# Spectral and attention layers in turn: table load, key maximum and value evictions rearranged at the end of the projections, and constant matmuls added there and in attention's first six steps

## The chip, the cores and the metric

The kernel runs on one core of a Trainium2 chip. The metric is the device time in microseconds (us) of one launch, from the first instruction to the last with what lies around it. Five engines work beside each other, each through its own instruction queue in order: TensorE (PE) multiplies matrices into PSUM, VectorE (DVE) and ScalarE (ACT) do elementwise work and carry PSUM into SBUF, GpSimd (POOL) does elementwise work in SBUF, and SyncE (SP) issues DMAs. They wait for each other by semaphores.

## The reference

The input `x` has 2048 rows of 512. Four layers follow each other, A, B, A, B, each added to `x` after a layer norm. A is a spectral filter, B an attention of 32 query heads with one shared key head and value head of 16 columns:

```python
def _A_ref(x, w_r, w_i):
    X = rfft2(x.astype(float32)) * (w_r + 1j * w_i)
    return irfft2(X, s=(S, D)).astype(bfloat16)

def _B_ref(x, wq, wk, wv, wo):
    q = (x @ wq).reshape(B, S, H, Dh).transpose(0, 2, 1, 3)
    k, v = x @ wk, x @ wv
    p = softmax(einsum("bhqd,bkd->bhqk", q, k) * Dh ** -0.5)
    o = einsum("bhqk,bkd->bhqd", p, v)
    return o.transpose(0, 2, 1, 3).reshape(B, S, H * Dh) @ wo

x = x + _A_ref(_layernorm(x), A_w_r, A_w_i)
x = x + _B_ref(_layernorm(x), B_wq, B_wk, B_wv, B_wo)
x = x + _A_ref(_layernorm(x), A_w_r, A_w_i)
x = x + _B_ref(_layernorm(x), B_wq, B_wk, B_wv, B_wo)
```

## The kernel before

The launch runs `spectral_layer` and `attention_layer` twice. `x` stays in SBUF as 16 tiles of 128 x 512, indexed (r, t).

**End of the spectral layer.** `back_s(t)` (L375) writes the four tiles of row block t: 16 matmuls of 128 x 512, an add to `x`, and a layer norm of two tiles at a time (L119), whose normalised tiles `xn_sb` come from ACT or POOL. The row blocks t = 0 to 3 are followed, one behind, by `block(t)` (L450), which makes the attention's inputs from row block t: 16 transposes in two halves into PSUM (L455), copied to `xT` by ACT (first half, L458) and DVE (second half, L460); four matmuls for the keys (L464), evicted to `KT` by ACT (L465); the largest absolute key per row, `kmax`, by DVE from `KT` (L466); 16 small matmuls for the values (L471), evicted four times, scaled, by ACT (L476) and DVE (L478) in turn. `block(0)` also makes the first two query groups. All its PSUM tiles come from one pool of two slots, `psum_b`, used in turn, so a tile waits until the tile two before it has been read. After `block(3)` comes `close` (L485): an exponential on one element (it makes ACT load its exponential table, L487), the maximum over the four `kmax` columns (L488), a scale (L489), and the scaling of all of `KT` in place in two pieces (L491).

**Attention.** The scores are made transposed: 128 keys by 512 queries per tile. A group g is 4 heads of one block of 512 queries; there are 32 groups of 64 score tiles. Each score matmul uses 32 rows of the array, one row strip per head (L569), and each product with the values 32 columns, one column strip per head (L681). Work is written out as 514 steps (L702). In a step, `dve_step` makes one score tile `dv` in PSUM, which DVE turns into integers (`t_new`, L693), and from step 4 on DVE also makes one image `s_new` of four tiles (L699); `act_step` makes three score tiles in one PSUM tile `sc` (two buffers, L663) and ACT takes the exponential of all three (`e`, L669); `pv_step` multiplies what was made two steps earlier with the values. `dv` has one PSUM buffer, so the next `dv` waits for the `t_new` before it. Group 0 takes 18 steps (17 of three tiles and one of one), later groups 16. Two steps after a group's end its sum is evicted by DVE (L584), and queries for the group after next are projected (L441, L446, L447).

**What sets the order.** Ahead of attention a scheduler orders each engine's instructions; within attention `chain` (L509) fixes the order as written. PE takes its instructions in that order, so a matmul that waits holds all behind it.

Of the kernel before, what the change touches and what calls it, by code (L numbers as in the profile page):

```python
# [9 lines left out]
ACT = mybir.ActivationFunctionType  # L10
ALU = mybir.AluOpType
P = 128
BF = mybir.dt.bfloat16
F32 = mybir.dt.float32
I32 = mybir.dt.int32
S, D, H, DH = 2048, 512, 32, 16
NF = D // 2 + 1
NT = 16
NC = 4
R = 4  # L20
T = 4
# [179 lines left out]
def spectral_layer(nc, tc, tabs, shared, lnpool, x_sb, xn_sb, WT, WX, aw, nxt, loads):  # L201
# [5 lines left out]
    with (tc.tile_pool(name="workA", bufs=1) as work,  # L207
# [210 lines left out]
        prep = attention_inputs(nc, tabs, shared, xn_sb, aw)  # L418
        for t in range(T):
            back_s(t)  # L420
            if t > 0:
                prep["block"](t - 1, psum_b)
        prep["block"](T - 1, psum_b)
        prep["close"](xn_sb[:, R - 1, T - 1, 0:1])
    return prep


def attention_inputs(nc, tabs, shared, xn_sb, aw):

    wq_sb, wka, wv_sb, vaug = aw["wq"], aw["wk"], aw["wv"], aw["vaug"]  # L430
    xT = [shared.tile([P, NC, 4, P], BF, tag=f"big{q}", bufs=1, name="xT") for q in range(NQB)]
    KT = shared.tile([P, S], BF, tag="KT", bufs=1)
    kmax = shared.tile([P, NQB], F32, tag="kmax", bufs=1)
    kb = shared.tile([P, 2], F32, tag="kb", bufs=1)
    xTq = [x.rearrange("d c t p -> d c (t p)") for x in xT]
    QT = {}

    def qproj(g, ps):
        qb, hg = divmod(g, HG)
        for c in range(NC):  # L440
            nc.tensor.matmul(ps, lhsT=wq_sb[:, c, hg, :], rhs=xTq[qb][:, c, :],  # L441
                             start=(c == 0), stop=(c == NC - 1))

    def qevict(ps):
        qt = shared.tile([P, 512], BF, tag="QT", bufs=3)
        nc.vector.tensor_copy(out=qt, in_=ps)  # L446
        nc.vector.tensor_tensor(out=qt.bitcast(I16), in0=qt.bitcast(I16), in1=tabs["QAND"], op=ALU.bitwise_and)  # L447
        return qt

    def block(t, psum):  # L450
        for half in range(2):
            ps = psum.tile([P, 2, NC, P], BF, tag="mm")
            for i in range(2):
                for c in range(NC):
                    nc.tensor.transpose(ps[:, i, c, :], xn_sb[:, 2 * half + i, t, c * P:(c + 1) * P], tabs["ident"])  # L455
            dst = xT[t][:, :, 2 * half:2 * half + 2, :].rearrange("d c i p -> d i c p")
            if half == 0:
                nc.scalar.copy(out=dst, in_=ps)  # L458
            else:
                nc.vector.tensor_copy(out=dst, in_=ps)  # L460
        ks = slice(t * 512, (t + 1) * 512)
        ps = psum.tile([P, 512], F32, tag="mm")
        for c in range(NC):
            nc.tensor.matmul(ps, lhsT=wka[:, c, :], rhs=xTq[t][:, c, :], start=(c == 0), stop=(c == NC - 1))  # L464
        nc.scalar.copy(out=KT[:, ks], in_=ps)  # L465
        nc.vector.tensor_reduce(out=kmax[:, t:t + 1], in_=KT[:, ks], axis=mybir.AxisListType.X,  # L466
                                op=ALU.max, apply_absolute_value=True)
        psv = psum.tile([P, 4, DH], F32, tag="mm")
        for i in range(4):
            for c in range(NC):  # L470
                nc.tensor.matmul(psv[:, i, :], lhsT=xT[t][:, c, i, :], rhs=wv_sb[:, c, :],  # L471
                                 start=(c == 0), stop=(c == NC - 1))
        for j in range(4):
            dst = vaug[:, j, 4 * t:4 * t + 4, 0:DH]
            if j % 2 == 0:
                nc.scalar.mul(out=dst, in_=psv, mul=PH_W[j])  # L476
            else:
                nc.vector.tensor_scalar(out=dst, in0=psv, scalar1=PH_W[j], scalar2=None, op0=ALU.mult)  # L478
        if t == 0:
            for g in range(2):  # L480
                ps = psum.tile([P, 512], F32, tag="mm")
                qproj(g, ps)
                QT[g] = qevict(ps)

    def close(xn_last):  # L485
        dmyo = shared.tile([P, 1], F32, tag="dmyo", bufs=1)
        nc.scalar.activation(out=dmyo, in_=xn_last, func=ACT.Exp)  # L487
        nc.vector.tensor_reduce(out=kb[:, 0:1], in_=kmax, axis=mybir.AxisListType.X, op=ALU.max)  # L488
        nc.vector.tensor_scalar(out=kb[:, 1:2], in0=kb[:, 0:1], scalar1=tabs["KAB"][:, 1:2], scalar2=None, op0=ALU.mult)  # L489
        for a, b in ((0, 512), (512, S)):  # L490
            nc.vector.tensor_scalar(out=KT[:, a:b], in0=KT[:, a:b], scalar1=tabs["KAB"][:, 0:1], scalar2=kb[:, 1:2],  # L491
                                    op0=ALU.mult, op1=ALU.add)

    return {"xT": xT, "KT": KT, "QT": QT, "qproj": qproj, "qevict": qevict, "block": block, "close": close}


def attention_layer(nc, tc, tabs, shared, lnpool, x_sb, xn_sb, aw, prep, nxt, store):
    with ExitStack() as ctx:
# [4 lines left out]
        xT, KT, QT = prep["xT"], prep["KT"], prep["QT"]  # L503
        qproj, qevict = prep["qproj"], prep["qevict"]

        mark, last = [None], {}
# [40 lines left out]
        for n0 in range(s0[NG]):  # L547
            lst = []
            if n0 in d_phase:
                g, b, j = d_phase[n0]  # L550
# [3 lines left out]
            n = n0 + LAG  # L554
# [9 lines left out]
        psp = ctx.enter_context(tc.tile_pool(name="psp", bufs=1, space=bass.MemoryType.PSUM))  # L564
        pv, tb, sb, ex, otc = {}, {}, {}, {}, {}

        def score(dst, g, kc, h):
            hs = slice(32 * h, 32 * h + 32)
            nc.tensor.matmul(dst, lhsT=KT[hs, kc * P:(kc + 1) * P], rhs=QT[g][hs, :], start=True, stop=True)  # L569
# [9 lines left out]
        def later(steps, fn):  # L579
            todo.setdefault(now[0] + steps, []).append(fn)  # L580

        def evict(g):
            o = work.tile([P, 512], F32, tag="oraw")
            nc.vector.tensor_copy(out=o, in_=pv.pop(g))  # L584
            d1 = dram.tile([4, 512], F32, tag="d1")
            nc.sync.dma_start(out=d1, in_=o.rearrange("(h r) q -> h r q", r=32)[:, 16, :])
            den = work.tile([P, 16], F32, tag="den")
            nc.sync.dma_start(out=den, in_=d1.rearrange("h (i c) -> (h i) c", c=16))
            return o, den
# [10 lines left out]
        def invert_later(g, o, den):  # L600
            rb = invert(den)
            later(6, lambda: normalise(g, o, rb))
# [57 lines left out]
        def act_step(n):  # L660
            if n >= s0[NG]:
                return
            sc = psc.tile([P, 3, 512], F32, tag="sc")  # L663
            for i, (g, kc, h) in enumerate(act_tiles[n]):
                score(sc[:, i, :], g, kc, h)
            na = len(act_tiles[n])
            e = work.tile([P, 3, 512], BF, tag="e", bufs=7)
            ex[n] = e
            nc.scalar.activation(out=e[:, 0:na, :], in_=sc[:, 0:na, :], func=ACT.Exp, scale=SCALE)  # L669
# [15 lines left out]
        def dve_step(n):  # L685
            if n in d_score:
                g, kc = d_score[n]
                dv = psd.tile([P, 512], F32, tag="dv")
                score(dv, g, kc, kc % 4)
                if kc % 4 == 0:  # L690
                    t_new = work.tile([P, 4, 512], I16, tag="T", bufs=3)
                    tb[(g, kc // 4)] = t_new
                nc.vector.tensor_scalar(out=tb[(g, kc // 4)][:, kc % 4, :], in0=dv, scalar1=T_MUL, scalar2=T_ADD,  # L693
                                        op0=ALU.mult, op1=ALU.add)
            if n in d_phase:
                g, b, j = d_phase[n]
                s_new = work.tile([P, 4, 512], I16, tag="S", bufs=7)
                sb[(g, b, j)] = s_new
                image[0] = nc.vector.tensor_scalar(out=s_new, in0=tb[(g, b)], scalar1=0.5, scalar2=16384.0 + PH_OFF[j],  # L699
                                                   op0=ALU.mult, op1=ALU.add)  # L700

        for n in range(s0[NG]):  # L702
            now[0] = n
            for fn in todo.pop(n, ()):
                fn()
            if n in evict_at:
                o, den = evict(evict_at[n])
                later(4, lambda g=evict_at[n], o=o, den=den: invert_later(g, o, den))
            dve_step(n)
            act_step(n)  # L710
            if n in qproj_at:
                ps = psp.tile([P, 512], F32, tag="pv")
                qproj(qproj_at[n], ps)
                later(1, lambda g=qproj_at[n], ps=ps: QT.__setitem__(g, qevict(ps)))
            else:
                pv_step(n)
            if nxt is not None and n in qproj_at and qproj_at[n] in (11, 15):
                nxt["load"](qproj_at[n] // 4 - 2)
            chain()
# [234 lines left out]
```

## Time and profile before

| | us |
|---|---|
| median of 3 runs (lowest to highest) | 1675.91 (1675.52 to 1676.21) |
| the profiled execution | 1673.17 |
| its span, first to last instruction | 1671.4 |
| PE busy in the span | 1421.6 (85%) |
| DVE busy | 1551.7 (93%) |
| ACT busy | 1505.6 (90%) |
| POOL busy | 158.4 (9%) |
| first score matmul of the first attention | 122.98 |
| first score matmul of the second attention | 947.67 |

All other times in this document that name a moment count from the start of the span. A matmul's shown duration holds its latency; four in a row on PE overlap. An engine's row in the chart of slices is its busy share in tenths, and PEclk is the TensorE clock that was granted, in tenths of full speed.

### The profile page before, as it was taken

The page shows a single profiled execution, that of the slowest core. Times are in us where ns is not written, and L with a number is a line of the kernel's source. Part 1 is how long each engine was busy: PE and PEld are TensorE (multiplying, and loading weights), DVE is VectorE, ACT ScalarE, POOL GpSimd, SP SyncE. Part 2 cuts the span into 40 slices and gives each one's busy share as a digit, 9 for nine tenths or more (in the row PEclk, how much of TensorE's full clock was granted, in tenths as well). Part 3 has the DMA queues.
Part 4 walks back from the last instruction along what each step waited for, and adds up shares of the span by engine and source line. Part 5 has one row for each costly group of instructions (what it writes and reads, how often), then busy time and mean ns, then how long its engine had stood idle before and what let it go on. Part 6 is the DMA issues. An engine that isn't in the chain of part 4 may idle for free.

```text
span 1671.4 us, 32246 instructions
## 1 busy us (share of the span) xinstructions
PE 1421.6 (85%) x12756; PEld 459.7 (28%) x12756; DVE 1551.7 (93%) x2796; ACT 1505.6 (90%) x1250; POOL 158.4 (9%) x264
## 2 busy tenths in 40 slices
PE   7889888888888888888988798888888888888887
PEld 2331222222222222222333322222222222222222
DVE  6877999999999999999878689999999999999994
ACT  4358999999999999999843699999999999999994
POOL 3210000000000000000111100000000000000000
PEclk9896999999999999999999789999999999999999
DMA  7000000000000010000020000000000000000002
GB/s 276 2 1 4 14 16 17 17 16 17 17 17 16 16 29 16 17 17 28 24 70 1 1 8 17 17 16 17 17 16 16 17 15 15 14 16 17 16 17 65
DMA packets 47880, 40.26 MB, mean 24 GB/s; under 512 B 30832, under 2 KB 36208, under 8 KB 47472
## 3 DMA queue, kind: packets, MB, share of 16 engines
q1 hardware_dynamic: 47728, 38.19, 7.7%
q8 instruction: 100, 1.64, 0.4%
q14 instruction: 52, 0.43, 0.1%
HBM read 33.04 MB, written 3.15 MB: 22 GB/s over the span
## 4 chain that ended last, share of the span: by engine, by line
DVE 39%; ACT 24%; PE 18%; issue 17%; DMA 1%; POOL 1%; SPq 0%; POOLq 0%; DVEq 0%; ACTq 0%
ACT e L669 23%; DVE t_new L693 15%; DVE s_new L699 12%; PE pv_new L681 6%; PE dv L569 3%; PE sc L569 2%; DVE o L584 2%; DVE qt L446 2%; PE fd L275 2%; DVE qt L447 2%; PE ps L192 1%; DVE stats L125 1%; PE ps L367 1%; PE ps L379 1%; DVE den L592 1%
## 5 line engine op out<-in xcount | busy, mean ns | idle before, releaser
L669 ACT ACTIVATE e<-sc 128x1536 bf16<-128x1536 f32 (+1 forms) x1028 | 1386.4, 1526 | 16.0 <-PE sc L569 15.5
L693 DVE TENSOR_SCALAR t_new<-dv 128x512 int16<-128x512 f32 x1016 | 695.0, 684 | 35.8 <-PE sc L569 14.5
L699 DVE TENSOR_SCALAR s_new<-t_new 128x2048 int16<-128x2048 int16 x1016 | 698.3, 688 | 0.0
L569 PE MATMUL dv<-qt,KT 32*128 32x512 bf16 x1016 | 389.2, 383 | 121.8 <-DVE t_new L693 114.0
L569 PE MATMUL sc<-qt,KT 32*128 32x512 bf16 x3080 | 421.6, 389 | 36.5 <-ACT e L669 3.2
L681 PE MATMUL pv_new<-s_new,vaug 128*32 128x512 bf16 x4064 | 412.0, 393 | 27.0 <-DVE qt L446 27.0
L681 PE MATMUL pv_new<-e,vaug 128*32 128x512 bf16 x3080 | 408.7, 385 | 0.4 <-ACT e L669 0.4
L569 PEld LDWEIGHTS <-KT 32*128 32x128 bf16 x4096 | 201.2, 91 | 730.1 <-issue 714.9
L681 PEld LDWEIGHTS <-vaug 128*32 128x32 bf16 x7144 | 135.6, 94 | 276.1 <-issue 262.5
L625 POOL TENSOR_TENSOR ot_new<-o,rb 128x176 bf16<-128x176 f32 (+1 forms) x96 | 55.7, 582 | 706.8 <-DVE s_new L699 649.9
L625 POOL TENSOR_TENSOR od<-o,rb 128x176 bf16<-128x176 f32 (+1 forms) x90 | 49.6, 551 | 597.6 <-DVE s_new L699 597.6
L441 PE MATMUL ps<-xT,wq_sb 128*128 128x512 bf16 x256 | 66.3, 381 | 10.8 <-DVE o L584 10.8
L275 PE MATMUL fd<-X,tab_DT 128*128 128x512 bf16 x256 | 56.1, 379 | 2.8 <-DVE X L242 2.8
L279 ACT CAST xn_sb<-fd 128x512 bf16<-128x512 f32 x32 | 18.8, 586 | 40.7 <-PE fd L275 40.7
L446 DVE CAST qt<-ps 128x512 bf16<-128x512 f32 x64 | 44.2, 691 | 0.8 <-PE ps L441 0.8
L584 DVE COPY o<-pv_new 128x512 f32<-128x512 f32 x64 | 43.8, 684 | 0.1
L367 PE MATMUL ps<-tab_PS,st 128*128 128x512 bf16 x128 | 32.8, 416 | 13.0 <-DVE st L315 12.0
L373 ACT CAST U<-ps 128x512 bf16<-128x512 f32 x24 | 14.1, 587 | 29.8 <-PE ps L367 29.8
L125 DVE BATCH_NORM_STATS2 stats<-x_sb 128x6 f32<-128x512 bf16 x48 | 31.8, 677 | 7.2 <-ACT x_sb L383 3.7
L441 PEld LDWEIGHTS <-wq_sb 128*128 128x128 bf16 x256 | 24.6, 96 | 39.7 <-issue 16.0
L275 PEld LDWEIGHTS <-tab_DT 128*128 128x128 bf16 x256 | 24.8, 98 | 32.8 <-issue 3.6
L379 PE MATMUL ps<-U,IT 128*128 128x512 bf16 x128 | 33.2, 379 | 0.0
(133 smaller groups left out, 567.2 us busy)
## 6 DMA issues: line engine op xcount, KB each, us to landing
rb<-d SPq DMA_DIRECT2D x256, 64.0 KB
FT<-const_FT SPq DMA_DIRECT2D x8, 512.0 KB
IT<-const_IT SPq DMA_DIRECT2D x8, 512.0 KB
x_sb<-in_A_x_dram SPq DMA_DIRECT2D x4, 512.0 KB
out_dram<-x_sb SPq DMA_DIRECT2D x16, 128.0 KB
ot_new<-od SPq DMA_DIRECT2D x120, 16.0 KB
wr_raw<-in_A_w_r_dram SPq DMA_DIRECT2D x1, 1028.0 KB
wi_raw<-in_A_w_i_dram SPq DMA_DIRECT2D x1, 1028.0 KB
```

The source lines that it names most:

```text
L275: nc.tensor.matmul(pss[i], lhsT=DT[:, b, w, 128 * fb:128 * fb + 128], rhs=X[:, b, part, c, :, :].rearrange("p k j -> p (k j)"), start=(b = ...
L367: nc.tensor.matmul(ps, lhsT=st[c][:, t, vec, q, fb, :], rhs=PS[:, fb, w, :], start=(k == 0), stop=(k == 3))
L379: nc.tensor.matmul(ps, lhsT=IT[:, t, part, c, r * P:(r + 1) * P], rhs=U[:, t, part, c, :], start=(k == 0), stop=(k == 3 and r % 2 == 1))
L441: nc.tensor.matmul(ps, lhsT=wq_sb[:, c, hg, :], rhs=xTq[qb][:, c, :], start=(c == 0), stop=(c == NC - 1))
L446: nc.vector.tensor_copy(out=qt, in_=ps)
L569: nc.tensor.matmul(dst, lhsT=KT[hs, kc * P:(kc + 1) * P], rhs=QT[g][hs, :], start=True, stop=True)
L584: nc.vector.tensor_copy(out=o, in_=pv.pop(g))
L625: pace(nc.gpsimd.tensor_tensor(out=dst[:, a:b], in0=o[:, a:b], in1=rb[:, a:b], op=ALU.mult))
L669: nc.scalar.activation(out=e[:, 0:na, :], in_=sc[:, 0:na, :], func=ACT.Exp, scale=SCALE)
L681: nc.tensor.matmul(pv[g][32 * h:32 * h + 32, :], lhsT=vaug[:, max(j, 0), kc, :], rhs=rhs, start=(first_pv[(g, h)] == u), stop=(last_pv[(g, ...
L693: nc.vector.tensor_scalar(out=tb[(g, kc // 4)][:, kc % 4, :], in0=dv, scalar1=T_MUL, scalar2=T_ADD, op0=ALU.mult, op1=ALU.add)
L699: image[0] = nc.vector.tensor_scalar(out=s_new, in0=tb[(g, b)], scalar1=0.5, scalar2=16384.0 + PH_OFF[j], op0=ALU.mult, op1=ALU.add)
```

## The change

In `block`, the maximum over the keys reads the PSUM tile, not the SBUF copy. `close` moves into `block(3)`, ahead of the value evictions, and its table-loading exponential reads a piece of `xT` that ACT has copied, in place of the last normalised tile. In `block(3)` a helper `filler` issues matmuls of the identity with data that lies there, into a PSUM tile that nobody reads: 6, 6 and 12. In attention's steps 1 to 5, 4, 3, 3, 2 and 2 such matmuls are written into the `sc` tile just ahead of the three score matmuls that overwrite it, and after step 1 four more into a `pv` tile. The core of the diff:

```diff
         for t in range(T):
             back_s(t)
             if t > 0:
                 prep["block"](t - 1, psum_b)
-        prep["block"](T - 1, psum_b)
-        prep["close"](xn_sb[:, R - 1, T - 1, 0:1])
+        prep["block"](T - 1, psum_b, psum)
...
+    def filler(psum, rhs, n):
+        ps = psum.tile([P, 512], F32, tag="pa", name="idle")
+        for _ in range(n):
+            nc.tensor.matmul(ps, lhsT=tabs["ident"], rhs=rhs, start=True, stop=True)
+
+    def close(last):
+        dmyo = shared.tile([P, 1], F32, tag="dmyo", bufs=1)
+        nc.scalar.activation(out=dmyo, in_=last, func=ACT.Exp)
...
-    def block(t, psum):
+    def block(t, psum, psum_idle=None):
+        if psum_idle is not None:
+            filler(psum_idle, xn_sb[:, 0, t, :], 6)
...
             if half == 0:
                 nc.scalar.copy(out=dst, in_=ps)
+                if psum_idle is not None:
+                    filler(psum_idle, xT[t][:, 0:2, 0:2, :], 6)
...
-        nc.vector.tensor_reduce(out=kmax[:, t:t + 1], in_=KT[:, ks], axis=mybir.AxisListType.X,
+        nc.vector.tensor_reduce(out=kmax[:, t:t + 1], in_=ps, axis=mybir.AxisListType.X,
                                 op=ALU.max, apply_absolute_value=True)
...
+        if psum_idle is not None:
+            filler(psum_idle, xTq[t][:, 0, :], 12)
+        if t == T - 1:
+            close(xT[t][:, NC - 1, 0:1, 0])
         for j in range(4):
             dst = vaug[:, j, 4 * t:4 * t + 4, 0:DH]
...
             sc = psc.tile([P, 3, 512], F32, tag="sc")
+            for _ in range((0, 4, 3, 3, 2, 2)[n] if n < 6 else 0):
+                nc.tensor.matmul(sc[:, 0, :], lhsT=tabs["ident"], rhs=KT[:, 0:512], start=True, stop=True)
             for i, (g, kc, h) in enumerate(act_tiles[n]):
                 score(sc[:, i, :], g, kc, h)
...
             dve_step(n)
             act_step(n)
+            if n == 1:
+                idle = psp.tile([P, 512], F32, tag="pv", name="idle")
+                for _ in range(4):
+                    nc.tensor.matmul(idle, lhsT=tabs["ident"], rhs=KT[:, 0:512], start=True, stop=True)
```

More of the change, by code (lines that the diff above doesn't have):

```diff
@@ L448, in qevict @@
         return qt
-    def block(t, psum):
+    def filler(psum, rhs, n):
[5 more added lines that the diff above has]
+        nc.scalar.activation(out=dmyo, in_=last, func=ACT.Exp)
+        nc.vector.tensor_reduce(out=kb[:, 0:1], in_=kmax, axis=mybir.AxisListType.X, op=ALU.max)
+        nc.vector.tensor_scalar(out=kb[:, 1:2], in0=kb[:, 0:1], scalar1=tabs["KAB"][:, 1:2], scalar2=None, op0=ALU.mult)
+        for a, b in ((0, 512), (512, S)):
+            nc.vector.tensor_scalar(out=KT[:, a:b], in0=KT[:, a:b], scalar1=tabs["KAB"][:, 0:1], scalar2=kb[:, 1:2],
+                                    op0=ALU.mult, op1=ALU.add)
+    def block(t, psum, psum_idle=None):
+        if psum_idle is not None:
+            filler(psum_idle, xn_sb[:, 0, t, :], 6)
         for half in range(2):
@@ L483, in block @@
                 QT[g] = qevict(ps)
[L485 to L494, printed above, removed]
+    return {"xT": xT, "KT": KT, "QT": QT, "qproj": qproj, "qevict": qevict, "block": block}
 def attention_layer(nc, tc, tabs, shared, lnpool, x_sb, xn_sb, aw, prep, nxt, store):
```

## The prediction

> **What bounds the kernel now.** I read the chart of slices first. All but the edges of both attentions is a wall of nines on DVE and ACT. The clock row dips in the second slice, in the fourth (125 to 167 us) and in the 23rd and 24th (919 to 1003); the fourth holds the first attention's first steps, the last two the second's:
>
> ```profile
> DVE  6877999999999999999878689999999999999994
> ACT  4358999999999999999843699999999999999994
> ...
> PEclk9896999999999999999999789999999999999999
> ```
>
> Next I asked for stretches around that dip and the one where the second attention begins. Columns: stretch and length; busy time of PE, its weight loads, DVE, ACT and POOL, each with its instructions; granted clock.
>
> ```profile
> 67.61:71.03 3.42, 2.72 (x7) 1.04 (x8) 3.35 (x10) 1.17 (x2) 0.00 (x0) 0.50 0.00 0
> 115.40:118.81 3.41, 1.12 (x13) 0.67 (x11) 1.27 (x4) 2.15 (x4) 0.00 (x0) 1.00 0.02 5
> 132.47:135.88 3.41, 3.41 (x22) 0.53 (x22) 2.48 (x4) 2.80 (x3) 0.00 (x0) 0.50 0.00 0
> 900.47:903.88 3.41, 1.57 (x6) 0.44 (x6) 3.34 (x11) 0.00 (x0) 0.00 (x0) 1.00 0.00 0
> 938.01:941.43 3.42, 1.14 (x26) 0.92 (x23) 1.04 (x3) 3.39 (x7) 0.67 (x1) 1.00 0.00 0
> 978.97:982.39 3.42, 3.13 (x16) 0.94 (x19) 2.63 (x6) 2.43 (x3) 0.00 (x0) 0.50 0.03 5
> ...
> 124.06:152.29 28.23, 27.57 (x148) 4.20 (x150) 16.56 (x27) 23.04 (x16) 0.00 (x0) 0.50 0.00 1
> 152.29:175.80 23.51, 18.97 (x187) 5.92 (x181) 22.43 (x38) 22.18 (x18) 2.10 (x3) 0.99 0.05 14
> 948.75:974.42 25.67, 24.99 (x152) 4.42 (x152) 17.04 (x27) 22.57 (x16) 0.00 (x0) 0.61 0.00 1
> 974.42:998.17 23.75, 20.11 (x180) 5.95 (x179) 22.01 (x37) 22.21 (x18) 1.66 (x3) 0.93 0.05 14
> 300.00:321.56 21.56, 18.54 (x181) 5.65 (x180) 21.32 (x37) 21.56 (x17) 1.65 (x3) 1.00 0.06 15
> ```
>
> The reader is to see: PE is busy 1.12 and 1.14 us in the stretches just before each drop; then it runs at half clock, from 118.81 to 152.95 and from 941.43 to 968.73 (each a mean of 0.50). Steady attention (300 to 321.56) takes 21.56 us for 16 steps with ACT full; nine of its exponentials in a row (from 184.04) span 12.19 us with a last one of 1.45, so a step is (12.19 - 1.45) / 8 = 1.34. In 132.47 to 135.88 PE itself is full: it is the bound there. The timeline shows what that costs:
>
> ```profile
> 115.05 1.28 ACT L487 ACT_TABLE_LOAD   x1
> 116.56 1.00 ACT L458 COPY xT<-ps 128x1024 bf16<-128x1024 bf16 x1
> 118.46 1.57 PE L464 MATMUL ps<-xT,wka 128*128 128x512 bf16 x4 [0.79 <-DVE xT L460]
> 122.98 0.60 PE L569 MATMUL dv<-qt,KT 32*128 32x512 bf16 x1 [2.54 <-DVE KT L491]
> ...
> 124.06 10.18 ACT L669 ACTIVATE e<-sc 128x1536 bf16<-128x1536 f32 x7 [2.30 <-PE sc L569]
> 134.80 1.45 ACT L669 ACTIVATE e<-sc 128x1536 bf16<-128x1536 f32 x1 [0.56 <-PE sc L569]
> 136.74 1.45 ACT L669 ACTIVATE e<-sc 128x1536 bf16<-128x1536 f32 x1 [0.48 <-PE sc L569]
> ```
>
> From step 7 ACT starts every 1.94 us and waits half a microsecond for PE each time. So two stretches outside steady attention can give time: the end of the projections and attention's first 16 steps.
>
> **Filler work.** Per attention 42 constant matmuls are added: 24 in the last block, 14 ahead of scores, 4 after step 1. Four queued 128x512 matmuls take 1.02 us at full clock and one alone 0.38 (L441), so one adds (1.02 - 0.38) / 3 = 0.214 us; at half clock four take 1.89 and one 0.60, hence 0.43.
>
> **The last block (first attention).** The order of the engines' instructions puts the fillers where PE waited, and moves the table load behind ACT's `xT` copy.
> - Four fillers stand ahead of block 2's keys (L464, 112.75). They read POOL's tile, ready at 111.61 + 0.77 = 112.38, so the keys start at 113.3, 0.55 late, done at 114.34. ACT was on another tile until 114.34 anyway: its eviction moves only to 114.40, ending 114.99.
> - The key maximum still waits for that ACT copy (the order shows it) and now holds the PSUM slot: 0.69 for the row of L466 gives 115.74. Block 3's first transposes move from 114.96 to 115.80; two of the first six fillers hide in that gap.
> - ACT copies them at 116.45 (116.56 before). The second half no longer waits for value evictions behind the table load: 116.45, not 117.06. Then the table load, 117.35 to 118.63, beside the next six fillers.
> - Those wait for ACT's copy: 117.50 to 118.78. Block 3's keys start at 118.80, not 118.46; at full clock they take 1.04, not 1.57, and end at 119.84, 0.2 earlier.
> - From there eviction, maximum and key scaling keep their 2.92 (120.06 to 122.98): first score at 122.80. The 12 fillers run from 120.1 to 122.7, hidden by 0.1; whatever pushes them later pushes the scores.
>
> So the first score comes 0.2 earlier; in the second attention, where those keys were all at half clock (1.89) and the chain from block 2's eviction to the first score was 947.67 - 938.48 = 9.19 instead of 8.64, it comes 0.2 + 0.55 = 0.7 earlier. DVE's order also changes in blocks 0 to 2, with the same instructions up to each `xT` copy: I take 0; the ends are one maximum either way, 0.7 per attention.
>
> **The first steps, at full clock, from the first score.** `dv` and three scores share a row strip, so step 0's exponential starts at 0.65 (0.21 + 0.38 + a hop of 0.05), not 1.08. `t_new` frees `dv` at 1.10. Step 1: `dv` at 1.15, four fillers to 2.23, scores done 2.61, exponential at 2.66. Four fillers to 3.31; step 2: `dv`, three fillers to 4.18, exponential at 4.61. Step 3: `dv` at 4.62, three fillers to 5.48, exponential at 5.95, and now ACT's own 1.34 is the limit again: step 4 at 7.29, step 16 at 7.29 + 12 x 1.34 = 23.37. Without fillers it would be 0.65 + 16 x 1.34 = 22.09, so I take 1.3 of the 3.9 us of fillers in 18 matmuls as exposed; the ends are 0 and 3.9.
>
> Before, step 16 came 1.08 + 28.23 = 29.31 after the first score and 1.08 + 25.67 = 26.75 in the second attention. From step 16 to step 33 the first attention needed 23.51 at full clock (DVE busy 22.43: a short step meets the first eviction); I keep that for both. The second needed 23.75. Gains: 29.31 - 23.37 = 5.9, and 26.75 + 23.75 - 23.37 - 23.51 = 3.6. With 0.2 and 0.7: **10.4 us**. After step 33 both kernels run alike, and nothing gives it back: ACT and DVE keep their steady pace. The profiled execution took 1673.17, 1.77 beside its span, and would take 1662.8; the runs' median is 2.74 above it, and 1675.91 - 10.4 = **1665.5**.
>
> **Does the clock hold?** By PE's streams (a 128-column transpose streams a quarter of 0.214), the weakest 3.41 us in my chain, 114.16 to 117.57, have 0.1 of values, 0.43 and 0.07 of fillers and 0.86 of transposes: 1.46 us or 43%. By the same count 115.40 to 118.81 had 23%, and 900.47 to 903.88, after which the clock stayed, 38%. From step 6 on there is steady work, 11 matmuls in 1.34 us, as in the hundreds of microseconds at 1.00.
>
> The longest PE wait in the row before the drop is 1.50 us (117.06). [...]
>
> **Rivals.**
> 1. The clock falls all the same and comes back soon, as after 67.61 to 71.03 and 978.97 to 982.39, two half-clock stretches of full-array work. Keys at 118.80 take 1.89, the 12 fillers 5.2, and the first score comes at 126.1: 3.1 late (2.6 in the second); then the steps as forecast: 1675.9 + 3.1 - 5.9 + 2.6 - 3.6 = 1672.1. Against it: the 43%. Chance 0.12.
> 2. Slower: the clock falls and stays, the fillers being load on PE at 0.43. To those 3.1 come, by the same step chain at half clock, exponentials at 1.08, 4.18, 8.05, 10.6, 12.75 and 14.9; step 5 came at 8.31 before: 6.6 more. 9.7 and 9.2 in the two: 1695. It decides from the point where the fillers' full stretches no longer lift the clock; for it speaks 132.47 to 135.88, against it the two stretches of rival 1. Chance 0.10.
> 3. Only one drop is averted, the other start as before: 1675.9 - 4.3 or - 6.1, near 1670.7. The second start differs only by its place in the clock's stretches. Chance 0.09.
> 4. The clock holds, but drops where group 1 begins, as at 978.97, and stays down as from 118.81: 34.1 / 1.94 = 17.6 steps of 0.6 each give back 10.6 in one: 1676.1. Against it: that drop lasted 3.4 us and cost 23.75 - 23.51 = 0.24. Chance 0.05.
>
> **How the numbers follow.** The forecast has 0.64. Its own ends: no exposed fillers and 0.7 per attention, 10.4 + 2.6 + 1.4 = 14.4, hence 1661.5; all exposed, 5.2 more, hence 1670.7. With rival 3 and half of rival 1 the range is 1661.5 to 1672. A change under 0.2% (3.4 us) can't be told from none here. Faster by more: forecast, rival 3 and half of rival 1, 0.79. Within: the rest of rival 1 and rival 4, 0.11. Slower: rival 2, 0.10.
>
> **What would show it.** PEclk 1.00 from 85 to beyond 180 and from 915 to beyond 990; block 3's keys in 1.04; exponentials 1.34 apart from step 4, with two wider gaps before (about 2); the first score within 1 us of 122.8. Wrong if a stretch at 0.50 remains in the first 16 steps, if the 12 fillers end after key scaling, or if blocks 0 to 2 come late.

## The result, and the profile after

The changed kernel takes 1663.22 us (median; lowest 1661.54, highest 1664.52), the kernel before 1675.72 beside it (1674.12 to 1676.21): a ratio of 0.9926, with a 95% interval of 0.9909 to 0.9944. The forecast was 1665.5, in a range of 1661.5 to 1672. The profiled execution took 1663.20 with a span of 1661.4; before, 1673.17 and 1671.4. The chart of slices of the changed kernel:

```profile
DVE  6978999999999999999778799999999999999995
ACT  4359999999999999999843699999999999999995
...
PEclk9899999999999999999999999999999999999999
```

PEclk is at nine in the fourth slice and in the 23rd and 24th, where it was 6, 7 and 8 before. The same stretches as in the prediction (busy time of PE, its weight loads, DVE, ACT and POOL with their instructions, then the granted clock, the share of the DMA engines and GB/s), moved to the new times:

```profile
115.33:118.74 3.41, 3.00 (x30) 1.57 (x28) 0.69 (x1) 2.49 (x5) 0.00 (x0) 1.00 0.00 0
...
121.74:145.72 23.98, 22.52 (x169) 6.41 (x170) 16.89 (x27) 21.91 (x17) 0.00 (x0) 1.00 0.00 1
145.72:168.45 22.73, 18.75 (x179) 5.85 (x179) 21.84 (x37) 22.23 (x19) 2.11 (x3) 1.00 0.05 15
...
966.35:989.08 22.73, 18.75 (x179) 5.85 (x179) 21.78 (x37) 22.23 (x18) 1.65 (x3) 1.00 0.05 14
```

The first row holds the place where the clock fell before: PE is busy 3.00 us in it, not 1.12. The other three are steps 0 to 16 of the first attention (23.98 us; 28.23 before) and steps 16 to 33 of both (22.73; 23.51 and 23.75 before). All are at clock 1.00.

Where the 10.0 us between the two spans went, counted from the first `back_s` matmul (L379) ahead of each attention: to the first score 35.60 became 35.37 in the first attention and 36.15 became 35.36 in the second; from there to step 33's exponential 52.82 became 47.36 and 50.50 became 47.36. That is 5.69 and 3.93, 9.62 together. The remaining 0.4 lies outside. The first `back_s` comes 1.67 earlier because the kernel before lost the clock for 3.4 us at 81.3 in the spectral layer and the changed one did not (of the runs below, the two that lost it there, e4 and e5, have it at 87.6 and 87.3, all others at 85.6 to 86.1). The stretch from step 33 to the second `back_s` is 2.19 longer, since the changed kernel lost the clock at 798.0 and 900.4: it takes 735.7 before, 736.2 in e6, which lost the clock at 795.8 alone, 737.4 to 737.6 in the runs that lost it between 898 and 912 alone, and 737.9 in the changed kernel. The rest of the second attention and the end are 0.88 shorter. The change adds and moves no instruction in these three.

### The profile page after: what moved, and what is told of

The parts are those of the page before. It is cut to its first block, busy times and chain, and to the rows that moved or that the text cites. A ratio compares the mean times of both kernels' runs of the same rounds, so it can differ in the third digit from the quotient of the medians.

```text
span 1661.4 us, 32326 instructions
## 1 busy us (share of the span) xinstructions
PE 1417.9 (85%) x12754; PEld 468.0 (28%) x12840; DVE 1549.5 (93%) x2796; ACT 1504.4 (91%) x1250; POOL 158.3 (10%) x264
## 4 chain that ended last, share of the span: by engine, by line
DVE 40%; ACT 25%; issue 17%; PE 17%; DMA 1%; POOL 0%; SPq 0%; POOLq 0%; DVEq 0%; ACTq 0%
ACT e L684 23%; DVE t_new L708 15%; DVE s_new L714 12%; PE pv_new L696 5%; PE dv L582 3%; DVE o L597 2%; DVE qt L445 2%; PE fd L275 2%; PE sc L582 2%; DVE qt L446 2%; PE ps L192 1%; DVE stats L125 1%; PE tri L660 1%; PE ps L367 1%; PE ps L379 1%
## 5 line engine op out<-in xcount | busy, mean ns | idle before, releaser
L582 PE MATMUL dv<-qt,KT 32*128 32x512 bf16 x1016 | 383.2, 377 | 117.2 <-DVE t_new L708 114.4
L582 PE MATMUL sc<-qt,KT 32*128 32x512 bf16 x3080 | 405.4, 382 | 37.8 <-ACT e L684 4.4
L696 PE MATMUL pv_new<-s_new,vaug 128*32 128x512 bf16 x4064 | 408.8, 389 | 27.3 <-DVE qt L445 27.3
L696 PE MATMUL pv_new<-e,vaug 128*32 128x512 bf16 x3080 | 402.6, 380 | 0.4 <-ACT e L684 0.4
L440 PE MATMUL ps<-xT,wq_sb 128*128 128x512 bf16 x196 | 62.3, 378 | 13.9 <-DVE o L597 10.7
L367 PE MATMUL ps<-tab_PS,st 128*128 128x512 bf16 x126 | 34.3, 432 | 11.5 <-DVE st L315 10.4
L668 DVE TENSOR_TENSOR x_sb<-tri,x_sb 128x512 bf16<-128x512 f32 x14 | 9.2, 684 | 26.4 <-ACT x_sb L666 26.4
```

What stands on the lines that cost most here:

```text
L367: nc.tensor.matmul(ps, lhsT=st[c][:, t, vec, q, fb, :], rhs=PS[:, fb, w, :], start=(k == 0), stop=(k == 3))
L696: nc.tensor.matmul(pv[g][32 * h:32 * h + 32, :], lhsT=vaug[:, max(j, 0), kc, :], rhs=rhs, start=(first_pv[(g, h)] == u), stop=(last_pv[(g, ...
```

## The experiments

A **filler** is one of the constant matmuls, a **start** the end of the projections with attention's first 16 steps. Each ratio is against the kernel before, on the same chip, with its 95% interval. "Lost" is where the profiled execution was at half clock in the starts and where group 1 begins (step 18), with its length.

| run | median | before | ratio | lost |
|---|---|---|---|---|
| e1_no_fillers | 1669.47 | 1673.05 | 0.9982 [0.9972, 0.9992] | 113.3 (30.7), 939.4 (27.3) |
| e2_fillers_only | 1664.07 | 1673.05 | 0.9944 [0.9930, 0.9957] | 970.5 (6.8) |
| e3_block_fillers | 1668.07 | 1673.05 | 0.9968 [0.9958, 0.9979] | 126.0 (17.1), 952.0 (17.1) |
| e4_step_fillers | 1668.79 | 1673.05 | 0.9978 [0.9961, 0.9996] | 115.5 (13.7), 938.1 (13.7) |
| e9_changed_again | 1662.93 | 1673.35 | 0.9935 [0.9919, 0.9951] | none |
| e5_quarter_array | 1664.36 | 1673.35 | 0.9941 [0.9926, 0.9956] | none |
| e6_five_in_steps | 1664.18 | 1673.35 | 0.9936 [0.9915, 0.9957] | none |
| e7_five_and_group_change | 1664.41 | 1673.35 | 0.9936 [0.9916, 0.9957] | 124.7 (20.5) |
| e10_quarter_rows | 1688.82 | 1673.08 | 1.0093 [1.0079, 1.0108] | 116.3 (41.0), 949.1 (44.4), 996.9 (3.4) |
| e11_three_after_step_0 | 1659.92 | 1673.08 | 0.9919 [0.9904, 0.9934] | none |
| e8_maximum_from_sbuf | 1664.21 | 1673.08 | 0.9948 [0.9932, 0.9965] | 971.7 (3.4) |

**The order alone.** The changed kernel with no filler:

```diff
-        prep["block"](T - 1, psum_b, psum)
+        prep["block"](T - 1, psum_b)
...
-            for _ in range((0, 4, 3, 3, 2, 2)[n] if n < 6 else 0):
-                nc.tensor.matmul(sc[:, 0, :], lhsT=tabs["ident"], rhs=KT[:, 0:512], start=True, stop=True)
...
-            if n == 1:
-                idle = psp.tile([P, 512], F32, tag="pv", name="idle")
-                for _ in range(4):
-                    nc.tensor.matmul(idle, lhsT=tabs["ident"], rhs=KT[:, 0:512], start=True, stop=True)
```

> The change without any constant matmul: only table load, key maximum and evictions moved. Theory (the constant matmuls keep the clock at 1.00, and that is the gain): the clock falls again near both attention starts, step 16 comes 28 us after step 0, and the time is that of the kernel before less the 0.6 us per attention that the moved copy brings: 1674.5 us, between 1672 and 1677. Rival (the order of the last block is what saves): 1663 to 1666 us, with the clock at 1.00 or not.

The clock falls in both starts, for 30.7 and 27.3 us. Step 16 comes 26.0 us after step 0 (28.2 and 25.7 before). The 1674.5 expected was worked out from 1675.72; the kernel before took 1673.05 beside this run, so the gain is 3.6, where 1.2 was expected. The moves alone are worth about 0.2%, a quarter of the whole. With the clock down their effect on the path cannot be told from where the half-clock stretch begins (113.3 here, 118.8 before), so that 0.2% is not all the order's own.

**The fillers alone.** The kernel before, its order kept (`close` behind `block(3)`, the maximum from `KT`), with the same 42 fillers per attention:

```diff
-        prep["block"](T - 1, psum_b)
+        prep["block"](T - 1, psum_b, psum)
         prep["close"](xn_sb[:, R - 1, T - 1, 0:1])
```

> The kernel before with all 42 constant matmuls per attention, nothing moved. Theory: the clock holds at 1.00 through both starts; the first score comes some 0.3 us later than in the changed kernel; 1664 us, between 1662 and 1667. Rival (the order of the last block is what saves): 1674 us or more, since the constant matmuls are then only load.

This gives 0.9944, most of the change. Both starts hold: the first score at +35.51 and +35.53, step 16 at 23.96 in both. The second attention lost the clock for 6.8 us where group 1 begins, which cost 24.75 - 22.73 = 2.0 us.

**The fillers of the block alone, and those of the steps alone.** e3 leaves out the fillers of the steps (the second and third part of e1's diff), e4 those of the block (its first part).

> The change with the 24 constant matmuls of the last block alone, none in attention's steps. If the steps' own matmuls, 0.43 to 0.64 us of PE streams per 1.34 us step, keep the clock once it is up: the 2.5 us that the step fillers expose in each attention come back, 1658 us, between 1657 and 1661. If the clock falls after all in steps 0 to 5: step 16 comes 26 us or more after step 0, and the time is 1667 to 1674 us.

> The change with the 18 constant matmuls in attention's steps alone, none in the last block. Theory: the clock falls before the first score as in the kernel before, the step fillers run at half clock (0.43 us each) and, being full-array work, lift the clock again within one or two stretches of 3.41 us: first exponentials 3 us or more apart, then 1.34; 1670 us, between 1666 and 1676. Rival (what matters is the work in the steps): the clock is at 1.00 from step 3 on and the time is within 1.5 us of the changed kernel.

With the block's fillers alone the first score comes at +35.36, as in the whole change, and the first six steps run at 1.33 to 1.35 us; then the clock falls in the steps, at 126.0 and 952.0. With the steps' fillers alone it falls at 115.5 and 938.1, ahead of attention, and is back after 13.7 us, within the fillers (one of e4's seven executions took 1678.32, at a mean granted clock of 0.976; the others have 0.984 to 0.987). Either half gives 0.2 to 0.3%; what the two give together needs both weak stretches filled.

e3 also shows that it is not PE's busy time that counts. Its stretch ahead of the second loss, and the one in which the clock was then down in the first attention:

```profile
948.57:951.98 3.41, 2.94 (x22) 0.88 (x21) 3.32 (x7) 3.41 (x4) 0.00 (x0) 1.00 0.00 0
125.95:129.37 3.42, 3.42 (x18) 0.65 (x16) 2.60 (x5) 3.42 (x4) 0.00 (x0) 0.50 0.00 0
```

PE is busy 2.94 of 3.41 us, and the clock falls at its end; in the kernel before it stayed after 900.47 to 903.88, with 1.57 busy. What differs is how much of the array is fed. In the timeline of e3's PE:

```profile
949.07 0.39 PE L582 MATMUL sc<-qt,KT 32*128 32x512 bf16 x3
949.40 0.40 PE L694 MATMUL pv_new<-e,vaug 128*32 128x512 bf16 x3
...
950.74 0.40 PE L694 MATMUL pv_new<-s_new,vaug 128*32 128x512 bf16 x4
```

A score matmul feeds 32 rows (32\*128 in the rows above) and three of them, in different row strips, run beside each other (0.39 for three; the one `dv` at 948.67 takes 0.37). A product with the values feeds all 128 rows and 32 columns (128\*32), and three or four of them share their time (0.40 for either).

**A quarter of the columns.** First theory: the share of the array's cells that work. The changed kernel again (e9), and with every filler cut to 32 of 128 columns:

```diff
-            nc.tensor.matmul(ps, lhsT=tabs["ident"], rhs=rhs, start=True, stop=True)
+            nc.tensor.matmul(ps[0:32], lhsT=tabs["ident"][:, 0:32], rhs=rhs, start=True, stop=True)
```

(the fillers in the steps in the same way).

> The changed kernel as it is, beside the next three on the same chip: 0.9926 of the kernel before, between 0.991 and 0.9945, clock at 1.00 through both starts and the first 16 steps.

> The changed kernel with each constant matmul cut to 32 of the array's 128 columns: as many, as long (512 columns of moving data, 0.21 us), but on a quarter of the array. Theory (the clock goes by the filled part of the array, not by how long PE is busy): it falls in both starts although PE is as busy as in the changed kernel, the matmuls then take 0.43 us each, and the time is that of the kernel before or worse, ratio 0.998 to 1.012. Rival (PE's busy time keeps the clock): as the changed kernel, ratio 0.9926.

The theory falls. The clock held in both starts and the time is as with whole fillers. This is e5's stretch in the first steps:

```profile
122.15:125.56 3.41, 2.84 (x17) 0.81 (x14) 2.09 (x4) 1.45 (x1) 0.00 (x0) 1.00 0.00 0
```

Counted over cells it holds 0.23, less than the 0.25 and 0.34 of e3's two stretches after which the clock fell (both as e6's expectation counts them).

**The theory that took its place: row share.** In the kernel before, the clock's row changes at 81.27, 84.68, 118.81, 152.95, 941.43, 968.73, 978.97 and 982.39: all whole numbers of 3.413 us apart (10 in the 34.13 from 84.68 to 118.81, 231 in the 788.48 from 152.95 to 941.43). For each stretch between two such points take the matmuls' streams (512 elements are 0.214 us at full clock and 0.43 at half, from queues of four: (1.02 - 0.38) / 3 and (1.89 - 0.60) / 3), each weighted by the rows that are fed out of 128; what runs side by side adds up, to 1 at most. In e3's 948.57 to 951.98 the 12 score matmuls give 12 x 0.214 / 4 = 0.64 and three shared sets of products 3 x 0.214 = 0.64: 1.28 of 3.41, 0.38. e5's stretch above has 0.57, at 0.23 of the cells. Over the 13 profiled executions of this study (the two kernels and the 11 runs) the clock fell 59 times, 13 of them at the program's end, each time after a share of at most 0.39; it stayed up after some 6000 stretches, all but six of them at 0.38 or more. It rose 59 times, each time after 0.72 or more, and stayed down some 130 times, all but one (0.77) after at most 0.72. PE's streams without the weight do not part the cases: drops after up to 0.58, stays from 0.33; rises from 0.77, stays at half clock up to 0.96.

**Fewer fillers.** One filler in each of steps 1 to 5 and none after step 1; then the same with two each in steps 18 and 19, where group 1 begins:

```diff
-            for _ in range((0, 4, 3, 3, 2, 2)[n] if n < 6 else 0):
+            for _ in range((0, 1, 1, 1, 1, 1)[n] if n < 6 else 0):
```

```diff
+            for _ in range({1: 1, 2: 1, 3: 1, 4: 1, 5: 1, 18: 2, 19: 2}.get(n, 0)):
```

> The changed kernel with one constant matmul in each of steps 1 to 5, five in place of 18. Without any, the stretches before the clock fell were filled to 25% and 34%; five add 0.21 us in each 1.34 us step, or 16 points, to about 41 and 50%. Theory (filled share, with a bound between 34 and 38%): the clock holds, step 16 comes 21.5 to 22 us after step 0 instead of 24.0, two times 2.0 to 2.5 us are saved against the changed kernel: ratio to before 0.990. If the clock falls: like the run without step fillers, ratio 0.9968.

> As the kernel before this one, with two constant matmuls more in each of steps 18 and 19, where the run with fillers alone lost its clock at the second start (filled share 28%) and the kernel before too. Theory: the clock holds there in every execution; where it held anyway, the four matmuls hide in PE's waits: ratio 0.9885 to 0.990, with less spread. Rival (steps 18 and 19 are tight, since a short step meets the first eviction): up to 0.9 us more per attention, ratio 0.991.

e6's executions spread from 1655.98 to 1667.24, with the median at 0.9936, not the 0.990 expected where the clock holds. The profiled one was the shortest: clock held, steps at 1.33 to 1.35 from the second on, step 16 after 21.54 us. In e7's the first start lost the clock (step 16 after 27.89) and the second held it (21.54). Its stretch before that loss and the one behind it:

```profile
121.32:124.73 3.41, 2.71 (x18) 0.58 (x13) 2.08 (x3) 2.90 (x3) 0.00 (x0) 1.00 0.00 0
124.73:128.14 3.41, 3.41 (x13) 0.62 (x12) 1.44 (x3) 2.79 (x2) 0.00 (x0) 0.50 0.00 0
```

PE is busy 2.71 of 3.41, but with scores: the row share is 0.34. In e6 the 3.41 us that begin at 121.0 have 0.33, the changed kernel's 0.53. Where the points of 3.41 us lie against the program differs between the profiled executions: from e1's first loss, at 113.3, to those of e10, e7 and e3 it is 3.0, 11.4 and 12.7 us, no multiples of 3.41, with the first `back_s` at 85.6 to 86.1 in all four. So a weak place that is hardly longer than one stretch is hit in some and missed in others. e6's spread agrees: the mean granted clocks of its six executions, from the shortest to the longest, are 0.995, 0.991, 0.989, 0.988, 0.986 and 0.985, and 0.010 of 1660 us is 33 us more at half clock (0.010 x 1660 / 0.5). In e7 the two executions of 1659 have 0.995 and 0.996, the four of 1664 to 1669 0.986 to 0.989, so the clock, which was expected to hold in every execution, held in two of six at most; these two took 0.991 of before, as the rival in its expectation has it. Where the clock was lost shows in the profiled executions alone; for the others it is argued. The four fillers of steps 18 and 19 cost 23.25 - 22.79 = 0.5 us.

**A quarter of the rows.** The run that parts row share from its rivals: the same fillers, as many and as long, from 32 rows and with all columns.

```diff
-            nc.tensor.matmul(ps, lhsT=tabs["ident"], rhs=rhs, start=True, stop=True)
+            nc.tensor.matmul(ps, lhsT=tabs["ident"][0:32, :], rhs=rhs[0:32], start=True, stop=True)
...
-                nc.tensor.matmul(sc[:, 0, :], lhsT=tabs["ident"], rhs=KT[:, 0:512], start=True, stop=True)
+                hs = slice(32 * act_tiles[n][0][2], 32 * act_tiles[n][0][2] + 32)
+                nc.tensor.matmul(sc[:, 0, :], lhsT=tabs["ident"][hs, :], rhs=KT[hs, 0:512], start=True, stop=True)
```

(the four after step 1 are fed from rows 0 to 31).

> The changed kernel with every one of its 84 constant matmuls fed from 32 of the 128 array rows (all 128 columns, the same 512 streamed elements, so the same 0.21 us of PE each; those ahead of scores use the row strip of the score that follows them). The constant matmuls' results are not used, so the computation is whole. Theory, row share (time in which moving data enters the array, weighted by the rows that get data): a filler now counts a quarter, the 3.4 us from 118.4 hold about 0.24 instead of 0.6, and the clock falls in both starts, at 119 to 125 and again near 940, and stays down until the group change, since nothing there reaches 0.72; the 18 fillers of the steps then cost 0.43 each with PE as the bound: step 16 comes 28 to 34 us after step 0, and the time is 1670 to 1690, that is 0.997 to 1.01 of before. Rival, PE busy at all: the fillers take as long as before, so the clock holds as in the changed kernel: 1663, 0.9935, step 16 at 24.0. Rival, columns that are driven: the same 0.9935.

The rivals fall: 1.0093, slower than before. Its clock row, and two stretches, the one ahead of the first loss and one within it:

```profile
PEclk9986999999999999999999769999999999999999
```

```profile
112.88:116.29 3.41, 2.44 (x28) 1.52 (x25) 1.74 (x4) 2.32 (x5) 0.00 (x0) 1.00 0.02 5
...
147.01:150.42 3.41, 3.41 (x21) 0.65 (x21) 2.60 (x5) 2.43 (x3) 0.00 (x0) 0.50 0.00 0
```

The first has PE busy 2.44 and a row share of 0.32; in the changed kernel no 3.41 us from 112 to 130 have less than 0.44. The loss came at 116.3, earlier than the 119 to 125 expected, since the six fillers ahead of block 3's keys count a quarter as well. In the second PE is full, and the clock stays at 0.50: a row share of 0.71. It came back only when a stretch reached 0.75, after 41.0 and 44.4 us. Counted from `back_s`, the first score is 4.3 us later than in the changed kernel (4.4 in the second attention), and step 16 comes 31.4 us after step 0.

**Fillers where PE waits.** In e6 PE idles 0.57 us ahead of step 1's `dv`, in the weak place. So: three fillers there, one in each of steps 1 to 5 and 16 to 19.

```diff
-            for _ in range((0, 4, 3, 3, 2, 2)[n] if n < 6 else 0):
+            for _ in range(1 if 1 <= n <= 5 or 16 <= n <= 19 else 0):
...
-            if n == 1:
+            if n == 0:
...
-                for _ in range(4):
+                for _ in range(3):
```

> The changed kernel's block kept; in attention one filler ahead of the scores of steps 1 to 5 and of steps 16 to 19, and three after step 0's scores, where PE waits 0.57 us for DVE anyway (changed kernel: 4, 3, 3, 2, 2 ahead of scores and four after step 1). Theory, row share: the two weak stretches, 0.32 of 3.4 us from 121 and 0.30 where group 1 begins, rise to about 0.5, so the clock holds at 1.00 in both starts and at the group change in every execution; nothing of the fillers is exposed: step 16 comes 21.5 us after step 0, step 33 22.7 to 23.0 later, a gain of 2.3 us per start on the changed kernel: 1656 to 1659, 0.989 to 0.991 of before. Rival, the clock does not go by row share: it is lost in some executions, as with one filler in each of steps 1 to 5 and none after step 0 (1656 to 1667 there), a median near 1664. Rival, the three fillers after step 0 delay step 1 by the 0.2 us each that they take: step 1's exponential at 2.2 instead of 1.58, 1657 to 1660.

It is the shortest of all medians, 0.9919, and its executions lie within 1658.23 to 1660.22, at mean granted clocks of 0.993 to 0.995. That agrees with the theory: no 3.41 us from 112 to 160 or from 930 to 980 has a row share under 0.41, wherever one begins. From the first score to step 33 both attentions take 45.78 us; the changed kernel 47.36. The intervals of the two ratios overlap, so that it beats the changed kernel rests on these 1.58 us per attention, and on executions that do not overlap: those of e9, beside which the kernel before took 1673.35 (1673.08 here), begin at 1662.18. The median is 1 us over the 1656 to 1659 that was expected, and the trace shows where. The three fillers delay step 1 by 0.13 (1.71 against 1.58), and the stretch from step 16 to 33 is 0.64 longer than in e6. Step 17 has one score tile only, so its exponential is short (0.73 us in the changed kernel's trace, 1.45 for three tiles) and the fillers of steps 16 and 17 are not covered; ACT's row shows the gap that follows:

```profile
146.69 5.48 ACT L684 ACTIVATE e<-sc 128x1536 bf16<-128x1536 f32 x4 [0.76 <-PE sc L582]
```

**The maximum from SBUF.** One operand of the changed kernel put back:

```diff
-        nc.vector.tensor_reduce(out=kmax[:, t:t + 1], in_=ps, axis=mybir.AxisListType.X,
+        nc.vector.tensor_reduce(out=kmax[:, t:t + 1], in_=KT[:, ks], axis=mybir.AxisListType.X,
```

> The changed kernel with one operand put back: the maximum over the keys reads the evicted keys (KT, SBUF) as before, not the PSUM tile. Theory: the maximum no longer holds the PSUM slot that block 3's first transposes wait for (0.57 us in the changed kernel's trace), and ACT's copy moves from 114.75 to the end of its eviction, but the maximum takes the longer way behind ACT's eviction of block 3's keys on either operand, so the chain to the first score is shorter by up to 0.57 per attention: 1662 to 1663.2, 0.993. Rival: the first score goes by ACT's and the fillers' order and comes at +35.4 as before: no difference that can be measured.

Both expectations miss: the first score comes at +35.97 in both attentions, 0.6 later. PE's timeline tells why:

```profile
113.21 0.61 PE L471 MATMUL ps<-tab_ident,xn_sb 128*128 128x128 bf16 x8
114.92 1.46 PE L453 MATMUL idle<-xT,tab_ident 128*128 128x512 bf16 x6 [1.10 <-ACT xT L474]
116.21 0.61 PE L471 MATMUL ps<-tab_ident,xn_sb 128*128 128x128 bf16 x8
```

Without the PSUM wait the first eight transposes do start early (113.21), but the scheduler now puts the six fillers, which wait 1.10 us for ACT's copy, ahead of the second eight. So the run changes the order as well as the wait, and does not price the wait by itself.

## Why the prediction was right

**The mechanism** was right: the time went into half-clock stretches at the two starts, the fillers keep the clock up (e2, which lost it in neither start, 0.9944), the order without them gives a quarter of the change at most (e1 0.9982). The clock is 1.00 through both starts, as forecast.

**The last block** came out as worked. In the changed kernel's timeline:

```profile
114.10 1.35 PE L471 MATMUL ps<-tab_ident,xn_sb 128*128 128x128 bf16 x16 [0.57 <-DVE kmax L484]
...
115.49 0.69 DVE L478 COPY xT<-ps 128x1024 bf16<-128x1024 bf16 x1 [0.79 <-PE ps L471]
...
115.81 1.46 PE L453 MATMUL idle<-xT,tab_ident 128*128 128x512 bf16 x6 [0.36 <-ACT xT L474]
...
117.10 0.81 PE L482 MATMUL ps<-xT,wka 128*128 128x512 bf16 x3
...
118.37 2.75 PE L453 MATMUL idle<-xT,tab_ident 128*128 128x512 bf16 x12
...
120.04 0.99 DVE L461 TENSOR_SCALAR KT<-KT,tab_KAB,kb 128x512 bf16<-128x512 bf16 x2
...
121.09 0.38 PE L582 MATMUL dv<-qt,KT 32*128 32x512 bf16 x1
```

Block 2's keys start 0.60 later after the first `back_s` than before (0.55 forecast). The transposes wait for the maximum that holds the PSUM slot, 28.38 after `back_s` (28.41). The pitch of a filler is (2.75 - 0.38) / 11 = 0.215 (0.214). The 12 are just hidden: the last one's 0.215 ends at 120.95, key scaling at 121.03, and the score starts 0.06 after that, as it did before (122.92 and 122.98). The six ahead of block 3's keys are not hidden. DVE's copy of the second half of `xT` ends at 116.18 and the keys start at 117.10, behind these six; in e1, without fillers, they start 0.06 after that copy ends (116.60 and 116.66). That is about 0.86 us in each attention. The prediction has it in its chain (keys at 118.80), though it counts only the steps' fillers as exposed. From `back_s` the first score came 0.23 and 0.79 earlier; 0.2 and 0.7 were forecast. That it stands at 121.09 and not near 122.8 is the 1.67 of the spectral layer.

**The first steps** held the first of two errors, of opposite sign. Step 0's exponential came at +0.65 as worked, but ACT's row then reads:

```profile
121.74 1.45 ACT L684 ACTIVATE e<-sc 128x1536 bf16<-128x1536 f32 x1 [1.88 <-PE sc L582]
123.97 1.45 ACT L684 ACTIVATE e<-sc 128x1536 bf16<-128x1536 f32 x1 [0.77 <-PE sc L582]
126.33 1.45 ACT L684 ACTIVATE e<-sc 128x1536 bf16<-128x1536 f32 x1 [0.91 <-PE sc L582]
128.05 8.49 ACT L684 ACTIVATE e<-sc 128x1536 bf16<-128x1536 f32 x6 [0.27 <-PE sc L582]
```

After the first score, steps 1, 2, 3 and 4 are at 2.88, 5.24, 6.96 and 8.47, not 2.66, 4.61, 5.95 and 7.29. Step 16 comes at 24.63, not 23.37: of the 3.9 us of fillers 24.63 - 22.09 = 2.5 are exposed, not 1.3. The term that was mis-sized is PE's time for a step:

```profile
124.82 0.39 PE L582 MATMUL dv<-qt,KT 32*128 32x512 bf16 x1
125.14 0.82 PE L678 MATMUL sc<-KT,tab_ident 128*128 128x512 bf16 x3
125.89 0.39 PE L582 MATMUL sc<-qt,KT 32*128 32x512 bf16 x3
126.21 0.40 PE L696 MATMUL pv_new<-e,vaug 128*32 128x512 bf16 x3
126.54 0.39 PE L582 MATMUL dv<-qt,KT 32*128 32x512 bf16 x1
```

From `dv` to the fillers it is 0.32, not 0.214; three fillers take 0.75, not 0.64; the scores and the products behind them 0.32 and 0.33. A start that follows a matmul of another shape comes 0.1 later than within a row of equals, four times a step, and the products were left out of the chain from step 2 on. Their sum is 1.72, the measured step, and with two fillers 1.51 (1.50 measured); both are above ACT's 1.34, so PE stays the bound to step 5, where the prediction had ACT back at step 4. With one filler it is 1.29, under 1.34: e6 and e11 show no loss from that.

**From step 16 to 33** the second: 22.73, not the 23.51 taken over from before. That row was called full clock, but it began at 152.29 while the half-clock stretch lasted to 152.95: step 18 came 0.32 later after step 16 than in the changed kernel, step 21 0.78 later, and from there the two are equal. DVE did more in it, too (22.43 busy against 21.84), being behind from the slow steps. The runs bear it out: where the clock was back 4.3 us or more before step 16 and no filler stands in these steps (e1, e4, e3's first attention), they take 22.72 or 22.73; in e3's second, where it was back 0.5 us before, 23.37. The 22.73 is 0.78 more gain in each attention than forecast.

**The sum:** 6.1 and 4.3 were forecast for the two starts, 5.69 and 3.93 measured. The two errors, 1.26 too little cost and 0.78 too little gain, leave 0.48 less gain in each; that they cancel so far is luck, as nothing ties them. The first scores, 0.03 and 0.09 earlier than forecast, give back 0.1. The medians differ by 12.5, because the execution of before that was profiled lay 2.6 below its median; against the 1673 of the other chips e9's gain is 10.4.

**Does the clock hold?** The weakest 3.41 us were counted at 43% by streams, all of them full-array work, for which row share and streams are the same; the trace has 0.44 there, and it held. For the steps the count by streams would have been wrong: it puts e3's 0.58 above a stretch of 0.38 that held, and the clock fell after it. That the work from step 6 on keeps the clock was right, but where group 1 begins the changed kernel has 3.41 us with a row share of 0.30, which the prediction did not see; what saved it there was where the stretches lay (0.44 and 0.39 in the profiled execution).

**The rivals.** None came in the changed kernel, but three came in the experiments. One start lost alone (rival 3) is e7. A drop where group 1 begins (rival 4) is e2 and e8 (and e10's second attention), at 2.0 and 23.88 - 22.73 = 1.15 us, not 10.6 (in the kernel before the drop at 978.97 cost 23.75 - 22.73 = 1.02, not 0.24): whole-row work stands there, and the clock was back after 6.8 and 3.4 us. Fillers that become load at half clock (rival 2) are e10: 1688.82, 15.7 over the kernel before, against 1695, or 19, for full-row fillers.

## What to carry to other kernels

In these runs PE's clock went by how many array rows were fed, not by how long PE was busy: with score matmuls of 32 rows PE was busy for 2.94 of 3.41 us and still lost the clock (e3), and quarter-column fillers held it as well as whole ones (0.9941 and 0.9935, no loss in either start). So where the clock row dips as here, count rows x streams in every stretch between its points (3.41 us here), at any phase, and put a few fillers of 128 rows where that is lowest and PE waits anyway: e11's twelve in the steps, three of them in a wait, kept the clock as the changed kernel's 18 did, for 1.58 us less in each attention. A filler that stands ahead of work which is ready costs its time even where PE is mostly idle, as the six ahead of block 3's keys did (0.86); no run here leaves those six out by themselves. When adding work to an engine's step, sum the step at the pace after a change of shape (0.32 here), and compare it with the pace of the engine that sets the end.

## What the runs showed of the hardware that was not expected

- The clock did not come back at the row share at which it was lost: in the 13 profiled executions it fell 59 times, each time after at most 0.39, and rose 59 times, each time after 0.72 or more. In e10's first start PE was busy for 3.18 us or more of each of eleven stretches of 3.41 us, with row shares of 0.27 to 0.71, and none lifted the clock from 0.50.
- Driven columns mattered little: fillers of 32 columns held the clock in both starts (e5, 0.9941), fillers of 32 rows did not (e10, 1.0093), though at full clock four of them take 1.02 us like four whole ones.
- The border is not sharp by this count: 0.38 was followed by a loss in e3 and by none in the kernel before, and six stretches from 0.32 to 0.37 kept the clock. The trace of the changed kernel has 12754 matmul records to 12840 weight loads, so some are missing; what else enters is open.
- In the changed kernel's first steps a matmul that follows one of another shape (rows x columns) starts 0.31 to 0.32 us after it, where equals follow at 0.214; no such pair of 512 elements each is closer than 0.30 at full clock in its trace.
